# A recurrence's chunk products spread over earlier steps, its inverses moved to GpSimd alone, and copies moved from ScalarE to VectorE

## The chip, the cores and the metric

The kernel runs on one core of one Trainium2 chip. The metric is device time in microseconds (us); the profile adds one profiled execution of the program. PE is TensorE, PEld its weight loads, DVE VectorE, ACT ScalarE, POOL GpSimd, SP SyncE.

## The reference

Two stages. A recurrence over 768 time steps for 4 x 8 heads of dimension 40, then a small attention with four experts over its output.

```python
state = zeros((B, H, D, D))                     # B 4, H 8, S 768, D 40
for t in range(S):
    y[t] = einsum('bhd,bhde->bhe', r[t], state)
    Sa = einsum('bhde,bhe->bhd', state, a[t])
    state = state * w[t][:, :, None, :] - einsum('bhd,bhe->bhde', Sa, b[t]) \
            + einsum('bhd,bhe->bhde', v[t], k[t])
# then: top-2 gating of 4 experts; per expert causal softmax attention of width 64
# on q, k, v projections of y (width 320), and an output projection; weighted sum
```

Arithmetic is float32.

## The kernel before

**Chunks, groups, units.** The 768 time steps are cut into 24 chunks of 32. Four chunks make a group W (0 to 5). A unit is one chunk of eight heads (g = 0 to 3), so a group has 16 units and the recurrence 96, u = 0 to 95. Inside a chunk the recurrence is solved with small matrices: chunk products of decayed k and b (tile KB) with decayed a (tile AB) give strictly triangular 32x32 matrices; for the b part an inverse of (1 + that matrix) is needed for each head and chunk, 32 heads x 4 chunks = 128 of them in one group, one to a partition.

**Preparation, `prep(i)`**, i = 4W + g, makes for group W and eight heads: `a`, `b`, `c`, `s` (two scans on VectorE and two small instructions), `x`, `y` (A times the decay into AB, 512 elements each; `X`, `Y` are the same on GpSimd), `k`, `l` (the same for KB; `p` does both on GpSimd), `m`, `n` (chunk products on TensorE into PSUM, eight matrix products each, and a masking multiply on VectorE, L280, into GL), `d`, `q` (A's copies from AB into GL, L273), `o` (a store of GL's rows to DRAM, `Ld`), and `w`, `v`, `e` (loads of the next i's EW, EA, EK). In GL a group's 16 columns n = 4p + c are four chunks c for four pairs of heads p: `m` makes chunks 0 and 1, `n` chunks 2 and 3. GL has two buffers, so group W's products overwrite those of group W-2, whose units still read them (s_g, L362). EW, EA, EK have one buffer each after i = 7, AB four, KB ten.

**Inverse, `invert(w)`**: `ld` (`L`) loads MT, and a second copy of rows 11 to 30 into LT, from Ld; `cp` (`C`) sets the diagonal; `step` is one elimination step j of 30: a multiply (L309) and an add (L311) over m rows and 31 - j columns, m being the rows before row j. Rows 0 to 10 (KP = 11) are GpSimd's (list `tp`), the rest VectorE's (list `td`); LT lets GpSimd read row j unchanged. `st` (`S`) stores MT to DRAM (Td, L313), `bk` (`R`) loads it transposed into TT (L316, four loads). The inverse of group 0 has a split of its own.

**Order.** Every engine runs its instructions in the order in which the code emits them. A loop over steps n emits seven slots, one stage each of another unit: u (of unit n-1, the first user of TT), g (n), y (n-3), f (n-2), t (every other step), k, v. f's product is masked by VectorE (L383), which y of the next step needs; `decay` (L402) follows after slot 3. Preparation and inverse are put between by hand, in the tables SIDE, SIDE1 and SIDE2: the key is the step relative to n0 = 16(W-1), the slashes count slots, "1s" is `s` of g = 1, "t2" two instructions of `td`, L, C, S, R the inverse's parts (S, R and t count from n0 + 16). So group W is prepared while the units of group W-2 run, and inverted while those of W-1 run; u of group W's first unit needs TT. `tp` is spread over steps n0 + 4 to n0 + 12 (POOLT; to n0 + 10 for W = 1). SyncE issues nearly all DMAs in that same order. PSUM tiles `ps` go round over four buffers for u, g, f, v and the chunk products. W = 0 and i < 8 are done by START and EARLY.

Of the kernel before, what the change touches and what calls it, by code (L numbers as in the profile page):

```python
# [7 lines left out]
F32 = mybir.dt.float32  # L8
AF = mybir.ActivationFunctionType
# [25 lines left out]
    -13: "///1abc",  # L35
    -12: "///1s t1 1x t1",
    -11: "///1y t3/t2//1w",
    -10: "///1k t1 1l t1///1ve",
    -9: "///t1 2ab t1 2c/t2",
    -8: "///t1 2s t2 2x/t2//2w",  # L40
    -7: "///t1 2y t3/t2//2v",
    -6: "///2k t1 2l t2///2e",
    -5: "///3ab t1 3c t2",
    -4: "///3skl t1///3w",
    -3: "/S//3X/0m//0nodq",
    -2: "/R//3y/1m//1nodq 3v",
    -1: "/3e///2m//2nodq",
    0: "////3m//3nodq",
    1: "L",
    3: "C",  # L50
}

SIDE1 = {
    -11: "///t1",
    -10: "t1",
    -9: "t3///t2/t2",
    -8: "//t1/t1/t1",
    -7: "/t2/t1/t1/t2",
    -6: "//t1//t2",
    -5: "t1/t1//t1///t2",  # L60
    -4: "t1/t1//t2",
    -3: "///S/t1",
    -1: "/R",
    2: "L",
    6: "C",
}
SIDE2 = {
    -15: "///0abcs///0w",
    -14: "/0kly//0X///0ev",
    -13: "//1a/1bc",  # L70
    -12: "///t1 1s t1//1x",
    -11: "/t1//t1/t2//1w",
    -10: "///t1 1kl/t2/1y/1e",
    -9: "//2a/t1 2bc t1 2s/1v//t1",
    -8: "//t1/t1 2x/t3//2w",
    -7: "///t1 2y t3/2v t2",
    -6: "///2l t2 2k t1///2e",
    -5: "/t1/3a/3bc t1",
    -4: "///3k t1 3s/t1",
    -3: "/S 3Xw//0n/0m//0qo 3l",  # L80
    -2: "/0d/R/3y/1m/1n/1d 2q 3v",
    -1: "1o////3m 2m//2ndo",
    0: "/3e/1q/3q/3n//3do",
    1: "L",
# [52 lines left out]

def recurrence(tc, ctx, I, xT, CM, early, tail=None, KP=(11, 11, 11, 11, 11, 11)):
    nc = tc.nc
# [6 lines left out]
    def ps(shape):  # L146
        return pp.tile(shape, F32, name="ps", tag="ps", bufs=4)
# [23 lines left out]
    MT = ring("MT", [128, 32, 32], 1)[0]  # L171
    TP = [sp.tile([128, n], F32, name=f"TP{k}") for k, n in enumerate((220, 130))]
    TF = ring("TT", [128, 1032], 2)
# [73 lines left out]
    def prep(i):  # L247
# [24 lines left out]
        def f5(s):  # L272
            A.activation(gl[64:104, g, :, s, :], AB[64 * s:64 * s + 40, :, 32 * s:32 * s + 32], AF.Copy)  # L273
        def mm(c):
            p_a = ps([64, 4, 2, 64])
            for p in range(4):
                for cc in range(2):
                    n = p * 4 + c + cc
                    T.matmul(p_a[:, p, cc, :], kb[0:104, n, :], AB[0:104, n, :], start=True, stop=True)  # L279
            V.tensor_tensor(gl[0:64, g].rearrange("q (p c) s t -> q p c s t", p=4)[:, :, c:c + 2].rearrange("q p c s t -> q p (c s) t"),  # L280
                            p_a.rearrange("q p c (s t) -> q p (c s) t", s=2), maskn[:, None, None, :].to_broadcast([64, 4, 4, 32]),
                            op=OP.mult)
# [3 lines left out]
        def load(k):  # L286
            load_e(i + 1, k)
        return dict(a=f0a, b=f0b, c=f0c, s=f1, x=lambda: f2(0), X=lambda: f2(0, PL), y=lambda: f2(1), Y=lambda: f2(1, PL), p=fp, k=lambda: fk(0), l=lambda: fk(1),
                    d=lambda: f5(0), q=lambda: f5(1), m=lambda: mm(0), n=lambda: mm(2), o=f6,
                    w=lambda: load(0), v=lambda: load(1), e=lambda: load(2))  # L290

    def invert(w):
# [3 lines left out]
        def ld():  # L296
            nc.sync.dma_start(M, Ld[w % 2])
            nc.sync.dma_start(L, Ld[w % 2][:, kp:31])
        def cp():
# [18 lines left out]
        for j in range(1, 31):  # L318
            if w:
                tp += step(PL, j, 0, kp, TP[0])  # L320
                td += step(V, j, kp, 32, TP[1])
            else:
                x, y = (step(V, j, r, q, (TP[1], flat(KB[8]))[k]) for k, (r, q) in enumerate(((0, KS), (KS, kp))))
                td += x[:1] + y[:1] + x[1:] + y[1:]
                tp += step(PL, j, kp, 32, TP[0])
# [645 lines left out]
```

## Time and profile before

| | |
|---|---|
| time, median of 3 runs | 692.9 us (690.95 to 693.21) |
| the profiled execution | 693.37 us, its span 691.6 us, granted clock 0.933 |
| PE / DVE / ACT / POOL busy | 85% / 74% / 71% / 49% of the span |
| recurrence, units 0 to 95 | from 81.6 us to about 435 us |
| ACT A's copies, L273 | 48, 627 ns each |
| DVE chunk masks, L280 | 48, 64x512, 677 ns each |
| DMA | 82.09 MB, mean 119 GB/s |

The chain that ended last, as the profile follows it, lies wholly in the second stage; for the recurrence one reads windows and waits. A window row gives us, then the busy time of each engine with its count of instructions, then the granted clock, the DMA engines' share and GB/s. A waits row gives who waited for whom, us in total, times, longest. A timeline row gives start, duration, engine, line, operation and tiles, and in brackets the idle time before it and what ended it.

### The profile page before, as it was taken

The page shows a single profiled execution, that of the slowest core. Times are in us where ns is not written, and L with a number is a line of the kernel's source. Part 1 is how long each engine was busy: PE and PEld are TensorE (multiplying, and loading weights), DVE is VectorE, ACT ScalarE, POOL GpSimd, SP SyncE. Part 2 cuts the span into 40 slices and gives each one's busy share as a digit, 9 for nine tenths or more (in the row PEclk, how much of TensorE's full clock was granted, in tenths as well). Part 3 has the DMA queues.
Part 4 walks back from the last instruction along what each step waited for, and adds up shares of the span by engine and source line. Part 5 has one row for each costly group of instructions (what it writes and reads, how often), then busy time and mean ns, then how long its engine had stood idle before and what let it go on. Part 6 is the DMA issues. An engine that isn't in the chain of part 4 may idle for free. (4 is left out here: it accounts for less than half of the span.)

```text
span 691.6 us, 22423 instructions
## 1 busy us (share of the span) xinstructions
PE 585.3 (85%) x8849; PEld 510.3 (74%) x8849; DVE 515.0 (74%) x1248; ACT 492.2 (71%) x1311; POOL 336.8 (49%) x512
## 2 busy tenths in 40 slices
PE   5540587899789879968999999889989989999995
PEld 5540576797678779868988878778878877887774
DVE  8899869867976997798583675578887597667651
ACT  4593278789768977977899999447576666676762
POOL 5575469518824981785183010045456255333731
PEclk8555589999999999999999999989999999999998
DMA  7750654498477639855725892422231202202101
GB/s 219 208 146 14 140 142 118 125 204 208 112 140 204 159 102 192 213 129 112 198 69 127 251 235 69 144 75 58 77 91 34 77 23 77 77 11 53 42 30 44
DMA packets 89994, 82.09 MB, mean 119 GB/s; under 512 B 54936, under 2 KB 73112, under 8 KB 89880
## 3 DMA queue, kind: packets, MB, share of 16 engines
q1 hardware_dynamic: 89736, 80.47, 45.7%
q8 instruction: 72, 1.18, 0.8%
q14 instruction: 42, 0.34, 0.2%
q10 hardware_dynamic: 144, 0.10, 0.0%
HBM read 60.10 MB, written 14.16 MB: 107 GB/s over the span
## 5 line engine op out<-in xcount | busy, mean ns | idle before, releaser
L819 POOL TENSOR_TENSOR P<-P,m 128x128 f32<-128x128 f32 (+2 forms) x96 | 87.7, 935 | 97.4 <-DVE m L815 46.8
L390 PE MATMUL py<-R,LS 128*40 128x80 f32 x1536 | 82.5, 239 | 27.5 <-DVE R L383 20.1
L311 POOL TENSOR_TENSOR MT<-MT,TP 128x84 f32<-128x84 f32 (+13 forms) x169 | 88.1, 522 | 13.2
L390 PEld LDWEIGHTS py<-R,LS 128*40 128x40 f32 x1536 | 62.0, 119 | 35.9 <-DVE R L383 18.1
L279 PE MATMUL ps<-AB,KB 104*64 104x64 f32 x768 | 63.9, 251 | 23.8 <-DVE AB L266 8.4
L808 ACT ACTIVATE P<-sc,m 128x128 f32<-128x128 f32 (+2 forms) x96 | 60.7, 633 | 26.7 <-DVE m L807 21.4
L279 PEld LDWEIGHTS ps<-AB,KB 104*64 104x64 f32 x768 | 58.9, 164 | 27.5 <-issue 10.4
L807 DVE TENSOR_REDUCE m<-sc 128x1 f32<-128x128 f32 (+2 forms) x96 | 59.4, 622 | 22.3 <-PE sc L800 20.8
L383 DVE TENSOR_TENSOR R<-ps,CM 64x256 f32<-64x256 f32 x96 | 39.6, 413 | 45.8 <-PE ps L382 45.0
L364 ACT ACTIVATE GT<-ps 32x160 f32<-32x160 f32 x192 | 56.4, 294 | 20.5 <-PE ps L362 16.4
L797 PE MATMUL sc<-ks,qs 128*128 128x384 f32 (+4 forms) x256 | 63.2, 348 | 5.5 <-ACT P L808 5.3
L382 PE MATMUL ps<-RB,VU 128*64 128x64 f32 x768 | 63.3, 227 | 4.4 <-ACT VU L378 3.5
L382 PEld LDWEIGHTS ps<-RB,VU 128*64 128x64 f32 x768 | 54.2, 141 | 8.6 <-ACT VU L378 8.3
L372 ACT ACTIVATE R<-ps 32x160 f32<-32x160 f32 x192 | 56.5, 294 | 5.0 <-PE ps L370 1.8
L309 POOL TENSOR_TENSOR TP<-LT,MT 128x220 f32<-128x220 f32 (+9 forms) x100 | 56.2, 562 | 7.8
L827 PE MATMUL pt<-CM,P 128*128 128x128 f32 x336 | 52.9, 279 | 1.2 <-ACT pt L833 1.1
L400 ACT ACTIVATE R<-py 40x160 f32<-40x160 f32 x144 | 42.7, 297 | 13.5 <-PE py L390 10.4
L355 ACT ACTIVATE LS<-pt 64x320 f32<-64x320 f32 x96 | 41.5, 432 | 12.3 <-PE pt L351 10.9
L418 ACT ACTIVATE LS<-pt 40x320 f32<-40x320 f32 x92 | 39.6, 431 | 14.5 <-PE pt L414 12.8
L370 PE MATMUL ps<-GT,TT 128*33 128x40 f32 x1536 | 49.4, 207 | 0.5 <-ACT GT L364 0.2
L797 PEld LDWEIGHTS sc<-ks,qs 128*128 128x128 f32 x256 | 41.0, 191 | 10.6 <-ACT P L808 9.4
L719 PE MATMUL pt<-xh,wq 128*128 128x384 f32 x192 | 43.5, 363 | 3.6 <-POOL xh L698 1.5
(150 smaller groups left out, 1431.5 us busy)
## 6 DMA issues: line engine op xcount, KB each, us to landing
RB<-in_RB SPq DMA_DIRECT2D x24, 320.0 KB
EK<-in_EK SPq DMA_DIRECT2D x18, 416.0 KB
ks<-ks SPq DMA_DIRECT2D x32, 192.0 KB
R<-in_VG SPq DMA_DIRECT2D x24, 208.0 KB
EW<-in_EA SPq DMA_DIRECT2D x18, 214.5 KB
R<-in_VT SPq DMA_DIRECT2D x48, 80.0 KB
R<-in_RT SPq DMA_DIRECT2D x24, 160.0 KB
xT<-XT SPq DMA_DIRECT2D x48, 80.0 KB
```

Of the source, the lines that this page charges most:

```text
L279: T.matmul(p_a[:, p, cc, :], kb[0:104, n, :], AB[0:104, n, :], start=True, stop=True)
L309: return [lambda: e.tensor_tensor(tmp, row[:, None, :].to_broadcast([128, m, n]), M[:, r0:r0 + m, j][:, :, None].to_broadcast([128, m, n]) ...
L311: lambda: e.tensor_tensor(o, o, tmp, op=OP.add)]
L364: A.activation(gt[32 * g:32 * g + 32, s::2], p_g[64 * s:64 * s + 32], AF.Copy)
L372: A.activation(hd(r2[32:64, 40 * h0:40 * h0 + 320], 40)[:, s::2], p_u[64 * s:64 * s + 32], AF.Copy, scale=-1.0)
L382: T.matmul(p_f[:, 2 * p:2 * p + 2], vu[:, p, :], rb[:, 4 * g + p, :], start=True, stop=True)
L390: T.matmul(py[64 * s:64 * s + 40, p], ls[:, h, :], m, start=True, stop=True, tile_position=(0, 64 * s))
L797: T.matmul(ps[:, c, 0:cw], QS[b][:, e, o], KS[b][:, e, z, k], start=(z == 0), stop=(z == 1 and not last), skip_group_check=True)
L807: V.tensor_reduce(m[:, 0, t:t + 1], ps[:, 0:ch, 0:cw], axis=AX.XY, op=OP.max, negate=True)
L808: later(DE, lambda: A.activation(pv, ps[:, 0:ch, 0:cw], AF.Exp, bias=m[:, 0, t:t + 1], accum_out=m[:, 1, t:t + 1]))
L819: PL.tensor_tensor(P[:, 0:n], P[:, 0:n], m[:, 3, t:t + 1].to_broadcast([128, n]), op=OP.mult)
L827: T.transpose(p[:, 128 * y:128 * y + 128], st["P"][t][:, 128 * c:128 * c + 128], ident)
```

## The change

- The tables: of each preparation, `n` is split into `N` (chunk 2) and `M` (chunk 3), each with four products and a mask of 256 elements instead of one of 512. `m` goes to steps -12, -10, -7, -4, `N` to -6 to -3, `M` to -3 to 0 (before: `m`, `n` at -3 to 0). Some other parts move by a step or two, and the loads of the next EW, EA and EK by one to four steps; `3X` (GpSimd) becomes `3x` (VectorE). SIDE2 becomes the same as SIDE but for two early steps.
- `KP` of groups 1 to 5 is 31: GpSimd does all rows; `td` is empty, all `t` entries go, LT is not loaded for them. `S` and `R` stand at -2 and -1.
- A's copies `d`, `q` are done by VectorE from i = 8 on, and stand before `o`.

```diff
--- before.py
+++ after.py
@@ -33,54 +33,41 @@
     -15: "/0p//0xY///0v",
     -14: "//////0e",
     -13: "///1abc",
-    -12: "///1s t1 1x t1",
-    -11: "///1y t3/t2//1w",
-    -10: "///1k t1 1l t1///1ve",
-    -9: "///t1 2ab t1 2c/t2",
-    -8: "///t1 2s t2 2x/t2//2w",
-    -7: "///t1 2y t3/t2//2v",
-    -6: "///2k t1 2l t2///2e",
-    -5: "///3ab t1 3c t2",
-    -4: "///3skl t1///3w",
-    -3: "/S//3X/0m//0nodq",
-    -2: "/R//3y/1m//1nodq 3v",
-    -1: "/3e///2m//2nodq",
-    0: "////3m//3nodq",
+    -12: "///1s 0m 1x///1w",
+    -11: "///1y 1k 1l///1ve",
+    -10: "///2a 1m 2bc",
+    -9: "///2s 2x///2w",
+    -8: "///2y 2k 2l///2ve",
+    -7: "///3a 2m 3bc",
+    -6: "///3s 0N 3x///3w",
+    -5: "///3y 1N 3k 3l///3ve",
+    -4: "///2N 3m",
+    -3: "///0M 3N 0dqo",
+    -2: "///S 1Mdqo",
+    -1: "/R//2Mdqo",
+    0: "///3Mdqo",
     1: "L",
     3: "C",
 }
 
-SIDE1 = {
-    -11: "///t1",
-    -10: "t1",
-    -9: "t3///t2/t2",
-    -8: "//t1/t1/t1",
-    -7: "/t2/t1/t1/t2",
-    -6: "//t1//t2",
-    -5: "t1/t1//t1///t2",
-    -4: "t1/t1//t2",
-    -3: "///S/t1",
-    -1: "/R",
-    2: "L",
-    6: "C",
-}
+SIDE1 = {-2: "///S", -1: "/R", 2: "L", 6: "C"}
 SIDE2 = {
     -15: "///0abcs///0w",
     -14: "/0kly//0X///0ev",
-    -13: "//1a/1bc",
-    -12: "///t1 1s t1//1x",
-    -11: "/t1//t1/t2//1w",
-    -10: "///t1 1kl/t2/1y/1e",
-    -9: "//2a/t1 2bc t1 2s/1v//t1",
-    -8: "//t1/t1 2x/t3//2w",
-    -7: "///t1 2y t3/2v t2",
-    -6: "///2l t2 2k t1///2e",
-    -5: "/t1/3a/3bc t1",
-    -4: "///3k t1 3s/t1",
-    -3: "/S 3Xw//0n/0m//0qo 3l",
-    -2: "/0d/R/3y/1m/1n/1d 2q 3v",
-    -1: "1o////3m 2m//2ndo",
-    0: "/3e/1q/3q/3n//3do",
+    -13: "///1abc",
+    -12: "///1s 0m 1x///1w",
+    -11: "///1y 1k 1l///1ve",
+    -10: "///2a 1m 2bc",
+    -9: "///2s 2x///2w",
+    -8: "///2y 2k 2l///2ve",
+    -7: "///3a 2m 3bc",
+    -6: "///3s 0N 3x///3w",
+    -5: "///3y 1N 3k 3l///3ve",
+    -4: "///2N 3m",
+    -3: "///0M 3N 0dqo",
+    -2: "///S 1Mdqo",
+    -1: "/R//2Mdqo",
+    0: "///3Mdqo",
     1: "L",
     2: "////C",
 }
@@ -135,7 +122,7 @@
     return {"CM": cm}
 
 
-def recurrence(tc, ctx, I, xT, CM, early, tail=None, KP=(11, 11, 11, 11, 11, 11)):
+def recurrence(tc, ctx, I, xT, CM, early, tail=None, KP=(11, 31, 31, 31, 31, 31)):
     nc = tc.nc
     ep = early.enter_context(tc.tile_pool(name="early", bufs=1, side="right"))
     sp = ctx.enter_context(tc.tile_pool(name="rec", bufs=1))
@@ -169,7 +156,7 @@
     GL = [t[:, 0:4096].rearrange("p (g n s t) -> p g n s t", g=4, n=16, s=2) for t in GF]
     LT = ring("LT", [128, 20, 32], 1)[0]
     MT = ring("MT", [128, 32, 32], 1)[0]
-    TP = [sp.tile([128, n], F32, name=f"TP{k}") for k, n in enumerate((220, 130))]
+    TP = [sp.tile([128, n], F32, name=f"TP{k}") for k, n in enumerate((240, 130))]
     TF = ring("TT", [128, 1032], 2)
     TT = [t[:, 0:1024].rearrange("p (n t) -> p n t", n=32) for t in TF]
     LS = ring("LS", [128, 32, 40], 2)
@@ -270,15 +257,19 @@
         def fk(k):
             V.tensor_tensor(kb[0:104, :, 32 * k:32 * k + 32], EK.rearrange("p (n k c) -> p n k c", n=16, k=2)[:, :, k], sv[:, :, 1:33], op=OP.mult)
         def f5(s):
-            A.activation(gl[64:104, g, :, s, :], AB[64 * s:64 * s + 40, :, 32 * s:32 * s + 32], AF.Copy)
-        def mm(c):
-            p_a = ps([64, 4, 2, 64])
+            o, x = gl[64:104, g, :, s, :], AB[64 * s:64 * s + 40, :, 32 * s:32 * s + 32]
+            if i < 8:
+                A.activation(o, x, AF.Copy)
+            else:
+                V.tensor_copy(o, x)
+        def mm(c, m=2):
+            p_a = ps([64, 4, m, 64])
             for p in range(4):
-                for cc in range(2):
+                for cc in range(m):
                     n = p * 4 + c + cc
                     T.matmul(p_a[:, p, cc, :], kb[0:104, n, :], AB[0:104, n, :], start=True, stop=True)
-            V.tensor_tensor(gl[0:64, g].rearrange("q (p c) s t -> q p c s t", p=4)[:, :, c:c + 2].rearrange("q p c s t -> q p (c s) t"),
-                            p_a.rearrange("q p c (s t) -> q p (c s) t", s=2), maskn[:, None, None, :].to_broadcast([64, 4, 4, 32]),
+            V.tensor_tensor(gl[0:64, g].rearrange("q (p c) s t -> q p c s t", p=4)[:, :, c:c + m].rearrange("q p c s t -> q p (c s) t"),
+                            p_a.rearrange("q p c (s t) -> q p (c s) t", s=2), maskn[:, None, None, :].to_broadcast([64, 4, 2 * m, 32]),
                             op=OP.mult)
         def f6():
             nc.sync.dma_start(Ld[w % 2][32 * g:32 * g + 32].rearrange("n j t -> j n t"),
@@ -286,7 +277,7 @@
         def load(k):
             load_e(i + 1, k)
         return dict(a=f0a, b=f0b, c=f0c, s=f1, x=lambda: f2(0), X=lambda: f2(0, PL), y=lambda: f2(1), Y=lambda: f2(1, PL), p=fp, k=lambda: fk(0), l=lambda: fk(1),
-                    d=lambda: f5(0), q=lambda: f5(1), m=lambda: mm(0), n=lambda: mm(2), o=f6,
+                    d=lambda: f5(0), q=lambda: f5(1), m=lambda: mm(0), n=lambda: mm(2), N=lambda: mm(2, 1), M=lambda: mm(3, 1), o=f6,
                     w=lambda: load(0), v=lambda: load(1), e=lambda: load(2))
 
     def invert(w):
@@ -295,7 +286,8 @@
         kp = KP[w]
         def ld():
             nc.sync.dma_start(M, Ld[w % 2])
-            nc.sync.dma_start(L, Ld[w % 2][:, kp:31])
+            if kp < 31:
+                nc.sync.dma_start(L, Ld[w % 2][:, kp:31])
         def cp():
             PL.memset(M.rearrange("p t j -> p (t j)")[:, ::33], 1.0)
         def step(e, j, r0, r1, tmp):
@@ -318,7 +310,6 @@
         for j in range(1, 31):
             if w:
                 tp += step(PL, j, 0, kp, TP[0])
-                td += step(V, j, kp, 32, TP[1])
             else:
                 x, y = (step(V, j, r, q, (TP[1], flat(KB[8]))[k]) for k, (r, q) in enumerate(((0, KS), (KS, kp))))
                 td += x[:1] + y[:1] + x[1:] + y[1:]
@@ -439,23 +430,14 @@
     for W in range(1, NW):
         n0 = 16 * (W - 1)
         inv = invert(W)
-        td = list(inv["td"])
-        if W == NW - 1:
-            spread(n0 + 3, n0 + 12, 3, td)
-            td = []
         for r, line in {1: SIDE1, 2: SIDE2}.get(W, SIDE).items():
             for k, part in enumerate(line.split("/")):
                 for z in part.split():
-                    fs = []
-                    if z[0] == "t":
-                        fs, td = td[:int(z[1:])], td[int(z[1:]):]
-                    elif z == "S":
-                        fs, td = td + [inv["st"]], []
-                    elif z in "LCR":
-                        fs = [inv[{"L": "ld", "C": "cp", "R": "bk"}[z]]]
+                    if z in "LCSR":
+                        fs = [inv[{"L": "ld", "C": "cp", "S": "st", "R": "bk"}[z]]]
                     else:
                         fs = [P[4 * W + int(z[0])][x] for x in z[1:]]
-                    at(n0 + r + (16 if z[0] in "tSR" else 0), k, *fs)
+                    at(n0 + r + (16 if z in "SR" else 0), k, *fs)
         p0, p1 = POOLT.get(W, POOLT[0])
         spread(n0 + p0, n0 + p1, 0, inv["tp"])
 
```

## The prediction

> **What bounds the kernel now.** I read the page first, then the span by stage, then single steps, then the instructions of GpSimd and the DMA queue. The profiled execution took 693.37 us; the runs shown have a median of 692.9, so the sum below, made against 693.37, stands 0.5 above it.
>
> ```profile
> span 691.6 us, 22423 instructions
> PE 585.3 (85%) x8849; PEld 510.3 (74%) x8849; DVE 515.0 (74%) x1248; ACT 492.2 (71%) x1311; POOL 336.8 (49%) x512
> ```
>
> No engine is full on average, so the stages decide. The recurrence runs 96 units, 16 to a group of four chunks. I cut the span at the first u product of groups 0 to 5. Rows: us, then busy time of PE, PEld, DVE, ACT, POOL.
>
> ```profile
> 81.60:147.40 65.80, 56.34 (x1150) 51.60 (x1150) 53.54 (x115) 48.49 (x139) 36.20 (x63) 0.90 0.56 132
> 147.40:211.70 64.30, 55.69 (x1184) 50.13 (x1184) 49.42 (x114) 51.02 (x146) 39.05 (x65) 0.97 0.70 165
> 211.70:272.20 60.50, 54.19 (x1189) 48.75 (x1189) 50.95 (x114) 50.88 (x145) 38.07 (x64) 1.00 0.65 157
> 272.20:334.10 61.90, 53.76 (x1189) 48.61 (x1188) 48.68 (x110) 50.84 (x145) 38.37 (x64) 1.00 0.68 162
> 334.10:383.50 49.40, 47.31 (x1060) 41.45 (x1058) 28.62 (x79) 45.59 (x136) 25.03 (x61) 1.00 0.52 127
> ```
>
> Group 4 prepares nothing for a later group and takes 49.4. Groups 0 to 3 take 11 to 16 more; that surplus is what the change can touch. Where it lies shows when group 3 is set beside group 4, the same steps in each (steps 7 to 11, then the last four):
>
> ```profile
> 293.00:313.10 20.10, 14.45 (x334) 13.04 (x332) 19.49 (x41) 15.65 (x48) 17.98 (x28) 1.00 0.57 137
> 313.10:334.10 21.00, 19.13 (x394) 17.73 (x394) 14.89 (x37) 16.11 (x42) 7.56 (x17) 1.00 0.60 129
> 354.90:371.30 16.40, 15.30 (x335) 13.24 (x333) 11.23 (x31) 15.38 (x47) 13.73 (x35) 1.00 0.23 60
> 371.30:383.50 12.20, 11.84 (x266) 10.36 (x264) 4.23 (x13) 11.13 (x34) 0.26 (x2) 1.00 0.82 173
> ...
> PE py L390 <- DVE R L383: 4.3, 4, 2.3
> PE ps L362 <- ACT R L372: 1.4, 1, 1.4
> ```
>
> Steps 7 to 11 cost 20.1 - 16.4 = 3.7 more: DVE is busy 19.49 of 20.10 and TensorE waits for its mask (4.3 in the group). The last four cost 21.0 - 12.2 = 8.8 more: all 64 chunk products lie there, and ScalarE, busy with A's copies, holds TensorE 1.4. Together 12.5 = 61.9 - 49.4.
>
> **The change, part by part.** Durations of group 3 by line:
>
> ```profile
> L309 DVE TENSOR_TENSOR TP<-MT 128x19 f32<-128x19 f32 (+9 forms) x19 | 7.3, 384 | 0.4
> L311 DVE TENSOR_TENSOR MT<-MT,TP 128x19 f32<-128x19 f32 (+9 forms) x19 | 7.1, 372 | 0.4
> L383 DVE TENSOR_TENSOR R<-ps,CM 64x256 f32<-64x256 f32 x16 | 6.6, 411 | 3.4 <-PE ps L382 3.2
> L266 DVE TENSOR_TENSOR AB<-EA,SC 40x512 f32<-40x512 f32 x6 | 5.0, 839 | 1.1 <-DMA EA<-in_EA 1.0
> L280 DVE TENSOR_TENSOR GL<-ps,CM 64x512 f32<-64x512 f32 x7 | 4.7, 679 | 3.5 <-PE ps L279 3.4
> ...
> L273 ACT ACTIVATE GL<-AB 40x512 f32<-40x512 f32 x24 | 14.8, 626 | 8.4 <-DVE AB L266 7.6 <-POOL AB L266 0.4
> L696 DVE CAST xh<-x 128x1152 fp32r<-128x1152 f32 x7 | 5.3, 756 | 0.4 <-DMA x<-xT 0.3
> ```
>
> *VectorE* loses 38 inverse instructions a group, 7.3 + 7.1 = 14.4. It gains eight of A's copies; no row shows one, so between 512/1152 of the cast (0.34) and the 512-element mask (0.68); I take 0.45, nearest the cast, as it too is a copy from SBUF: 3.6. It gains the third mask part, 0.68 + 2 x 0.41 for 2 x 0.68, 0.14 x 4 = 0.6, and one A product from GpSimd (3x), 0.84. Net -9.4. *ScalarE* loses 8 x 0.626 = 5.0, and the 1.4 stall goes. The next possible delay is VectorE's queue, where the copies stand before the next unit's mask; the last four steps have room (14.89 busy of 21).
>
> *TensorE* does the same 64 products. Eight cost about 1.1 (8 blocks, 8.8, the surplus above). Moved over ten steps they can fill idle time: two steps where ScalarE is relieved of R's copies take 5.4, two ordinary ones 6.4:
>
> ```profile
> 334.10:339.50 5.40, 5.40 (x137) 5.03 (x135) 3.20 (x9) 4.63 (x14) 0.00 (x0) 1.00 0.59 143
> 358.50:364.90 6.40, 5.99 (x135) 5.18 (x134) 4.77 (x13) 6.00 (x19) 5.42 (x13) 1.00 0.28 63
> ```
>
> So 0.5 a step is free, 4.3 over nine. Left to its units alone a prepared group would take 49.4 + 8.8 - 4.3 = 53.9. Bounds: 49.4 (all hidden) and 58.2 (none).
>
> *GpSimd.* The inverse of a group keeps 60 instructions, but rows 11 to 30 join. Elements summed over j of m(31-j): 7,260 before, 9,920 after, 2,660 more.
>
> ```profile
> 282.50 0.24 POOL L309 TENSOR_TENSOR TP<-MT 128x30 f32<-128x30 f32 x1
> 295.00 1.56 POOL L309 TENSOR_TENSOR TP<-LT,MT 128x220 f32<-128x220 f32 x1
> 301.52 0.87 POOL L311 TENSOR_TENSOR MT<-MT,TP 128x187 f32<-128x187 f32 x1
> 320.49 0.22 POOL L311 TENSOR_TENSOR MT<-MT,TP 128x11 f32<-128x11 f32 x1
> 342.06 0.25 POOL L309 TENSOR_TENSOR TP<-MT 128x30 f32<-128x30 f32 x1
> 352.22 0.58 POOL L309 TENSOR_TENSOR TP<-LT,MT 128x220 f32<-128x220 f32 x1
> 354.24 0.59 POOL L311 TENSOR_TENSOR MT<-MT,TP 128x209 f32<-128x209 f32 x1
> 356.76 0.55 POOL L311 TENSOR_TENSOR MT<-MT,TP 128x187 f32<-128x187 f32 x1
> 371.41 0.22 POOL L311 TENSOR_TENSOR MT<-MT,TP 128x11 f32<-128x11 f32 x1
> ...
> 294.95 1.25 DVE L257 TENSOR_TENSOR_SCAN SUF<-EW,D 104x528 f32<-104x528 f32 x1
> 301.17 0.82 DVE L266 TENSOR_TENSOR AB<-EA,SC 40x512 f32<-40x512 f32 x1
> ```
>
> Group 4, with no preparation beside it: 342.06 to 371.63 = 29.6. From 11 to 209 elements an instruction grows by 0.37, 1.85 ns an element: 2,660 cost 4.9, so 34.5 alone. Group 3 took 282.50 to 320.71 = 38.2, 8.6 more. The rows show why: beside a scan (294.95) an instruction takes 1.56 for 0.58, 1.0 more; beside an A product (301.17) 0.87 for 0.55, 0.32 more. Five scans and ten products of preparation lay in that window: 5.0 + 3.2 = 8.2. VectorE's own inverse parts, present in group 4 too, show no such cost, so I give nothing back for them. The new window starts earlier in the group and holds six scans and twelve products, 6.0 + 3.8 = 9.8, and some six copies; a copy costs 0 to 0.48 (0.68 less the 0.2 of a smallest instruction), I take 0.2: 1.2. Sum D = 34.5 + 9.8 + 1.2 = 45.5 in groups 1 to 3. In group 0 the first scan precedes the window and two copies fall in it: 34.5 + 5.0 + 3.8 + 0.4 = 43.7. In group 4, 34.5.
>
> The Trainium skill, GPSIMD Engine Reference, Engine selection, advises VectorE for elementwise work on a tile and puts GpSimd at about twice its time for two inputs. By that, with the 679 ns mask as VectorE's price (1.3 ns an element), the 2,660 elements would cost about 7 us for my 4.9, and four inverses 8 us more than my sum, an estimate from that page.
>
> *The queue around it.* SyncE's issues (start, us):
>
> ```profile
> 278.75 0.34 SPq L297 DMA_DIRECT2D MT<-Ld  x1
> 320.74 0.34 SPq L313 DMA_DIRECT2D Td<-MT  x1
> 323.51 2.20 SPq L316 DMA_DIRECT2D TT<-Td  x4
> 335.08 0.32 SPq L284 DMA_DIRECT2D Ld<-GL  x1
> 337.40 0.34 SPq L297 DMA_DIRECT2D MT<-Ld  x1
> ...
> 341.98 0.16 POOL L300 MEMSET MT<- 128x32 f32 x1 [20.15 <-DMA MT<-Ld]
> 92.87 0.24 POOL L309 TENSOR_TENSOR TP<-MT 128x30 f32<-128x30 f32 x1 [3.49 <-DMA MT<-Ld]
> ```
>
> From the inverse's end, TT's last load is issued 4.6 to 5.0 later (to 325.71); a load like MT's takes 3.5 (278.75 to 282.26) to 4.6, Td's round 2.8. TT is there at about +7.6 (7.3 to 9). Behind TT's loads in SyncE's queue stand the last groups' o stores, a chunk load, then 3o and L: 3o at +6, L 2.3 later, the inverse's start 3.5 to 4.6 after L. GpSimd starts the next inverse at +13 (12 to 14). The dropped LT load (320 KB) takes an issue out of that queue. The E loads move one to four steps sooner with the products that free their tiles, two steps ahead of their use as now, and past S and R: VectorE's 1.0 for EA may stay, and I count it as nothing. Behind S's wait stand 1o, 2o, 3o, R and chunk loads needed three or more steps later; only 3o and R are on the loop, and both are counted in the 13 and the 7.6. S is now passed at step -2 instead of -3; where the inverse ends later than that, it makes no difference.
>
> So the inverses form a loop of their own: period D + 13 = 58.5, against 53.9 for the units. Before, it was 38.2 + 13 = 51 and hidden. It is now what ends last. Times of the groups' starts: group 1 at 92.87 + 43.7 + 7.6 = 144.2 (was 147.4). Group 2: the inverse starts at 136.6 + 13 = 149.6, ends 195.1, TT 202.7 (211.7). Group 3: 208.1, 253.6, 261.2 (272.2). Group 4: 266.6, 312.1, 319.7 (334.1). In group 4: 325.1 + 34.5 + 7.6 = 367.2, before the units' 319.7 + 49.4 = 369.1 (383.5). Gain 14.4; the rest of the program moves along unchanged. 693.4 - 14.4 = **679**.
>
> **The rivals.** *A, the inverse stays hidden.* If D is under 41, units decide. For it: VectorE, rid of its parts, may reach its scans outside GpSimd's way. Against: five scans cost 5.0 whatever else runs. The time: groups 1 to 3 gain 10.4, 6.6 and 8.0 against 53.9, group 0 about 8 (half its surplus of 16.4, the half in its later steps), or 33: 660. *B, the slower side: the inverse on GpSimd alone grows past the old period.* Break-even is D = 62.2 - 13 = 49.2 (mean of groups 1 to 3). If each copy blocks like a scan (1.0, not 0.2), D is 50.3; with 0.9 ns an element more for long, narrow tiles, 52.7. Then group 1 starts 0.8 later, groups 1 to 3 lose 3.5 each and group 4 half a us: 693 + 12 = 705; by the copies alone 695. The Trainium skill, SBUF — State Buffer, Who interferes with whom, says that an fp32 copy on VectorE can hold the ports that it shares with GpSimd for the whole instruction. No row of this trace shows one beside GpSimd. *C, no difference*: D near 49 puts the TT wait just where the products lay; 690.8 to 695. *D, VectorE becomes full* in steps 3 to 10, where a scan, products and a mask stand in nearly every step: 3.0 to 3.4 a step (a scan 1.25, a product or two at 0.84, a chunk mask 0.68, the unit's own 0.7) beside 16.4/5 = 3.3 of unit time; it would cost 1 to 3 a group, hidden while the loop's 58.5 decides.
>
> **How the numbers follow.** Loop-bound as forecast (668 to 688): 0.55. A (655 to 668): 0.19. Small gain to 690.8: 0.05. C: 0.08. B: 0.13. Faster by over 0.3% (2.1 us, about what a measurement here can tell): 0.79; same 0.08; slower 0.13. Range 661 to 695: it leaves out A's lower end and B's upper, some 0.17.
>
> **What would show it.** Right: GpSimd's inverse lasting 45 in groups 1 to 3 and 34 in group 4; TensorE's u products at groups 2 to 4 waiting some 4 us for DMA TT<-Td; the waits for L383 and L372 gone; group 4 still 49.4. If u never waits for TT, A holds; if the inverse passes 49, B. The forecast is wrong also if TensorE waits for VectorE's masks in steps 4 to 11 longer than the 4.3 shown.

## The result and the profile after

The changed kernel takes 700.25 us (median of 9 runs, 696.02 to 703.48), the kernel before 693.21 (9 runs, 689.73 to 695.27). The ratio is 1.010, with an interval of 1.007 to 1.013: about 1% slower, where 2% faster was forecast. The profiled execution took 701.92 us. These two lines of its page stand against the two of before in the prediction; VectorE and ScalarE do less, GpSimd more, as the change says.

```profile
span 699.9 us, 22331 instructions
PE 587.9 (84%) x8849; PEld 513.8 (73%) x8849; DVE 475.3 (68%) x1110; ACT 471.8 (67%) x1279; POOL 366.4 (52%) x508
```

The same cut by groups (columns as before), and as a last row the end of group 3, its step 15:

```profile
81.70:147.80 66.10, 53.81 (x1149) 48.98 (x1150) 49.83 (x90) 44.72 (x133) 45.62 (x64) 0.91 0.54 129
147.80:212.10 64.30, 55.41 (x1184) 50.38 (x1184) 43.59 (x89) 45.82 (x136) 45.38 (x63) 0.92 0.66 156
212.10:275.00 62.90, 55.72 (x1184) 50.67 (x1184) 43.26 (x89) 45.80 (x136) 44.92 (x63) 0.93 0.61 154
275.00:337.80 62.80, 54.99 (x1184) 49.98 (x1184) 40.84 (x85) 45.81 (x136) 41.11 (x61) 0.93 0.59 145
337.80:391.80 54.00, 48.76 (x1056) 42.78 (x1057) 13.54 (x40) 45.81 (x136) 30.02 (x61) 0.97 0.42 111
...
327.90:337.80 9.90, 3.41 (x77) 3.12 (x76) 3.68 (x10) 3.50 (x10) 1.16 (x3) 0.81 0.79 147
```

Groups 0 to 4 took 66.1, 64.3, 62.9, 62.8 and 54.0, where they had taken 65.8, 64.3, 60.5, 61.9 and 49.4. Added up, the last group starts at 391.8 instead of 383.5, 8.3 later; the profiled executions differ by 8.55. More than half of it, 4.6, is in group 4, which prepares nothing. The last row shows where a prepared group loses time: the step before the next group's first unit takes 9.90, and TensorE works in 3.41 of them. The waits name the cause:

```profile
PE ps L361 <- DMA TT<-Td: 31.6, 5, 8.1
...
POOL MT L292 <- DMA MT<-Ld: 50.1, 5, 16.2
```

TensorE's u product waits 31.6 us for TT, 8.1 at most, once for each group 1 to 5. Behind it is the loop that was forecast: the inverse, the round over DRAM to TT, the last store, the load of MT, the next inverse. GpSimd, SyncE's queue and TensorE around the end of group 3 (timelines; start, duration):

```profile
283.66 0.24 POOL L301 TENSOR_TENSOR TP<-MT 128x30 f32<-128x30 f32 x1
328.97 0.26 POOL L303 TENSOR_TENSOR MT<-MT,TP 128x30 f32<-128x30 f32 x1
...
329.26 0.34 SPq L305 DMA_DIRECT2D Td<-MT  x1
329.70 0.38 SPq L275 DMA_DIRECT2D Ld<-GL  x1
332.05 2.31 SPq L308 DMA_DIRECT2D TT<-Td  x4
334.46 0.84 SPq L275 DMA_DIRECT2D Ld<-GL  x1
335.40 1.04 SPq L397 DMA_DIRECT2D xT<-XT  x2
336.53 0.60 SPq L325 DMA_DIRECT2D R<-in_VT  x1
337.22 0.37 SPq L275 DMA_DIRECT2D Ld<-GL  x1
...
340.05 0.71 SPq L288 DMA_DIRECT2D MT<-Ld  x1
...
337.83 0.42 PE L361 MATMUL ps<-GT,TT 128*33 128x40 f32 x6 [6.53 <-DMA TT<-Td]
345.39 0.16 POOL L292 MEMSET MT<- 128x32 f32 x1 [16.16 <-DMA MT<-Ld]
```

The inverse runs from 283.66 to 329.23, 45.57. S follows at once (329.26), the four TT loads of R at 332.05, and TensorE's u at 337.83, 8.6 after the inverse's end. Behind the TT loads SyncE issues 2o, two stores of xT, a load of tile R and 3o (337.22, 8.0 after the end), then L at 340.05 (10.8); the next inverse starts at 345.46, 16.2 after the end of the last.

Group 4 loses time at both ends. At its start TensorE works without a pause, but its first two steps take 6.80 where the same steps took 5.40 before (row 334.10:339.50 in the prediction): the granted clock is 0.77 of full speed in them, against 1.00.

```profile
337.80:344.60 6.80, 6.77 (x134) 6.38 (x135) 2.52 (x8) 3.75 (x12) 0.00 (x0) 0.77 0.78 203
```

In windows of one us the clock is 0.50 from 335 to 340, so it fell while TensorE waited for TT and came back about 3 us after TensorE had started again. That is 1.4 of the 4.6. At its end, group 4's inverse and queue read so:

```profile
379.76 0.27 POOL L303 TENSOR_TENSOR MT<-MT,TP 128x30 f32<-128x30 f32 x1
...
381.10 0.31 SPq L327 DMA_DIRECT2D R<-in_VT  x1
...
382.38 0.34 SPq L305 DMA_DIRECT2D Td<-MT  x1
387.46 2.14 SPq L308 DMA_DIRECT2D TT<-Td  x4
...
391.81 0.52 PE L361 MATMUL ps<-GT,TT 128*33 128x40 f32 x16 [3.10 <-DMA TT<-Td]
```

The inverse has ended at 380.03, but its store S is issued at 382.38, 2.35 later: in SyncE's queue it stands behind a chunk load that waits for y of step -2 (381.10) and two more. From S to the first TT load it takes 5.1, where 2.8 was enough in group 3, and u waits 3.10 for TT. With the 1.4 of the start this is 4.5 of the 4.6.

### The profile page after: what moved, and what is told of

Same layout as the page of the kernel before. It is cut to its first block, busy times and chain, and to the rows that moved or that the text cites. A ratio compares the mean times of both kernels' runs of the same rounds, so it can differ in the third digit from the quotient of the medians.

```text
span 699.9 us, 22331 instructions
## 1 busy us (share of the span) xinstructions
PE 587.9 (84%) x8849; PEld 513.8 (73%) x8849; DVE 475.3 (68%) x1110; ACT 471.8 (67%) x1279; POOL 366.4 (52%) x508
## 5 line engine op out<-in xcount | busy, mean ns | idle before, releaser
L801 POOL TENSOR_TENSOR P<-P,m 128x128 f32<-128x128 f32 (+2 forms) x96 | 87.6, 934 | 95.4 <-DVE m L797 51.1
L301 POOL TENSOR_TENSOR TP<-MT 128x84 f32<-128x84 f32 (+13 forms) x169 | 104.5, 618 | 18.3 <-DMA MT<-Ld 5.4
L303 POOL TENSOR_TENSOR MT<-MT,TP 128x84 f32<-128x84 f32 (+13 forms) x169 | 106.2, 629 | 13.2
L381 PE MATMUL py<-R,LS 128*40 128x80 f32 x1536 | 86.5, 242 | 5.6 <-DVE R L374 2.9
L270 PE MATMUL ps<-AB,KB 104*64 104x64 f32 x768 | 66.1, 253 | 24.0 <-DVE AB L253 7.9
L270 PEld LDWEIGHTS ps<-AB,KB 104*64 104x64 f32 x768 | 61.0, 167 | 26.3 <-issue 9.1
L363 ACT ACTIVATE R<-ps 32x160 f32<-32x160 f32 x192 | 56.5, 294 | 34.8 <-PE ps L361 31.6
L361 PE MATMUL ps<-GT,TT 128*33 128x40 f32 x1536 | 50.0, 211 | 31.6 <-DMA TT<-Td 31.6
L381 PEld LDWEIGHTS py<-R,LS 128*40 128x40 f32 x1536 | 65.3, 121 | 12.9 <-ACT LS L409 5.6
L373 PE MATMUL ps<-RB,VU 128*64 128x64 f32 x768 | 65.2, 230 | 5.1 <-ACT VU L369 4.1
L361 PEld LDWEIGHTS ps<-GT,TT 128*33 128x33 f32 x1536 | 37.6, 117 | 40.9 <-issue 32.8
L373 PEld LDWEIGHTS ps<-RB,VU 128*64 128x64 f32 x768 | 54.8, 143 | 10.8 <-ACT VU L369 9.6
L809 PE MATMUL pt<-CM,P 128*128 128x128 f32 x336 | 51.9, 276 | 2.3 <-ACT pt L815 1.8
```

The source lines that it names most:

```text
L301: return [lambda: e.tensor_tensor(tmp, row[:, None, :].to_broadcast([128, m, n]), M[:, r0:r0 + m, j][:, :, None].to_broadcast([128, m, n]) ...
L303: lambda: e.tensor_tensor(o, o, tmp, op=OP.add)]
L361: T.matmul(p_u[64 * s:64 * s + 33, p], tt[:, o:o + 33], gt[:, h, :], start=True, stop=True, tile_position=(0, 64 * s))
L363: A.activation(hd(r2[32:64, 40 * h0:40 * h0 + 320], 40)[:, s::2], p_u[64 * s:64 * s + 32], AF.Copy, scale=-1.0)
L373: T.matmul(p_f[:, 2 * p:2 * p + 2], vu[:, p, :], rb[:, 4 * g + p, :], start=True, stop=True)
L381: T.matmul(py[64 * s:64 * s + 40, p], ls[:, h, :], m, start=True, stop=True, tile_position=(0, 64 * s))
```

## Experiments

Theory 1 is the forecast's: the loop of inverse and queue ends last, and its parts add up. Its rivals differ from run to run: that VectorE or the units' own time decides, that the other parts of the change cost the time, and, from the fifth run on, theory 2: that the place of S and R in SyncE's queue does. All edits are against the changed kernel, but for the second one. D is the time of an inverse, E its end.

### The parts, each without another

**The inverse split again** between GpSimd and VectorE, all else as changed.

```diff
-def recurrence(tc, ctx, I, xT, CM, early, tail=None, KP=(11, 31, 31, 31, 31, 31)):
+def recurrence(tc, ctx, I, xT, CM, early, tail=None, KP=(11, 11, 11, 11, 11, 11)):
...
+                td += step(V, j, kp, 32, TP[1])
...
+        spread(n0 + 4, n0 + 13, 3, inv["td"])
```

> Everything as in the changed kernel, but the inverses of groups 1 to 5 are shared again (rows 0 to 10 GpSimd, 11 to 31 VectorE, VectorE's part spread evenly over steps n0+4 to n0+13). Theory 1 (the loop of inverse and its DMA rounds ends last, about 16.4 + D a group): GpSimd's inverse falls from 45.6 to about 40.5, TensorE's waits for TT fall from 31.6 in all to under 12, time 678 to 688. Rival (the spread products and VectorE's copies are what costs): time stays at 698 or above, with VectorE's mask as what TensorE waits for.

Measured: 732.66 against 691.96, ratio 1.058 (1.051 to 1.065). GpSimd's part fell to 37.3 to 38.9 in groups 0 to 3, yet S came 8.5 to 15.2 after its end, waiting for VectorE's part. Waits, and the window of group 3:

```profile
PE ps L270 <- DVE KB L258: 27.4, 10, 3.7
297.10:368.60 71.50, 59.64 (x1184) 54.79 (x1185) 52.52 (x123) 45.81 (x136) 33.53 (x62) 0.88 0.55 133
```

The early products need their KB, which VectorE makes, in steps where rows of the inverse stand in its queue. The time is the rival's, but TensorE waits for KB, and for TT 18.0, not for masks. The miss is one of theory 1's: shortening GpSimd's part does not shorten the loop when VectorE's part ends it. Only this even spread of VectorE's part was tried.

**The inverse on GpSimd alone in the kernel before**, its products, copies and queue unchanged.

```diff
-def recurrence(tc, ctx, I, xT, CM, early, tail=None, KP=(11, 11, 11, 11, 11, 11)):
+def recurrence(tc, ctx, I, xT, CM, early, tail=None, KP=(11, 31, 31, 31, 31, 31)):
...
-            nc.sync.dma_start(L, Ld[w % 2][:, kp:31])
+            if kp < 31:
+                nc.sync.dma_start(L, Ld[w % 2][:, kp:31])
...
-                td += step(V, j, kp, 32, TP[1])
```

> The kernel before with one part of the change alone: groups 1 to 5 inverted by GpSimd alone, the products at steps -3 to 0 and A's copies on ScalarE as before. Theory 1: D about 43 (34.5 alone, 8.6 for scans and products beside it), a loop of about 60 a group against groups of 60 to 64 before, so part of what VectorE gains is kept: 681 to 690, TensorE waiting 1 to 4 for TT in a group. Rival (GpSimd's longer inverse is a loss in itself): 698 or above.

Measured: 713.66, ratio 1.030 (1.024 to 1.037), the rival's side. D is 45.8, 46.9, 46.5, 43.2, 34.6. Its waits:

```profile
PEld ps L279 <- POOL AB L266: 21.6, 7, 6.1
PE ps L279 <- POOL AB L266: 14.4, 5, 5.9
```

The product 3X, which the change gives to VectorE, here stands behind the longer inverse on GpSimd; the last products and with them L come late, and the next inverse starts 19 to 22.7 after E. So the parts of the change need each other: either alone, placed as here, costs 3 to 6%.

### The terms of D

**One scan of each preparation left out** (the first of the two, SUF, of i = 8 and later; run twice, and D is read in the second run).

```diff
         def f0a():
+            if i > 7:
+                return
             V.tensor_tensor_scan(SUF[:, 0:528][:, ::-1], EW[:, ::-1], d1[:, ::-1], 1.0, op0=OP.mult, op1=OP.add)
```

> The changed kernel without the first scan (L257 of before, SUF) from i = 8 on; the later instructions read what the tile held, so outputs differ. Theory 1 with the port between VectorE and GpSimd as the price of D: three scans fewer in each window at 1.0 each, D 45.6 -> 42.6, and the loop passes it on: each of groups 1 to 3 and group 0 2 to 3 shorter, 688 to 692. Rival (the inverse's length is its instructions alone, or TensorE's wait has another cause): D stays at 45 or the time within 2 of the changed kernel.

> The kernel without the first scan from i = 8 on once more (later instructions read what the tile held, so outputs differ), for a profile of GpSimd's inverse. If VectorE's scans beside it lengthen it by 1.0 each, D of groups 1 to 3 is 42.6 to 43.5 against 45.6 to 46.5; if not, 45 or above.

Measured: 689.43 and 690.26, ratios 0.9964 (0.9933 to 0.9994) and 0.9985 (0.9953 to 1.0017). Both times lie in theory 1's range. D fell to 42.4, 42.9, 41.8, 42.3, by 3.2 to 4.2 for three scans beside an inverse (four in group 1), 0.9 to 1.4 each: about the 1.0 that the forecast read from one row. Group 4, without scans, kept 34.55. TensorE still waits 21.7 for TT.

**A's copies back on ScalarE**, at their new places.

```diff
-            if i < 8:
+            if i < 24:
                 A.activation(o, x, AF.Copy)
```

> The changed kernel with A's copies back on ScalarE. Theory 1: a copy on VectorE costs GpSimd's inverse 0 to 0.2, four to six of them stand in a window, so D falls by 0.3 to 1.0 and the time by 0 to 4: 696 to 700. Rival (a copy holds GpSimd like a scan, 1.0 each): D falls by 4 or more and the time by 12 or more.

Measured: 701.57, ratio 1.012 (1.007 to 1.017), no different from the change whole. D fell by 1.3, 1.0, 1.0 and 1.8, 1.3 in the mean, which for six copies would be the 0.2 each of the forecast. But in two of these four inverses one scan fewer also stands beside GpSimd. The changed kernel's rows show less: GpSimd goes on beside a copy, and its instructions lose little against those of the same size in group 4 (the last row).

```profile
327.90 0.87 DVE L264 COPY GL<-AB 40x512 f32<-40x512 f32 x2
...
327.92 0.57 POOL L303 TENSOR_TENSOR MT<-MT,TP 128x58 f32<-128x58 f32 x1
379.04 0.31 POOL L303 TENSOR_TENSOR MT<-MT,TP 128x58 f32<-128x58 f32 x1
```

This pair, 0.26, is the largest loss; beside the six copies of group 3 the losses add up to some 0.6, 0.1 each. Rival B's 1.0 each is excluded either way.

### Where the rest of the loop is

**Elimination steps 21 to 30 left out**, in groups 1 to 5.

```diff
-                tp += step(PL, j, 0, kp, TP[0])
+                tp += step(PL, j, 0, kp, TP[0]) if j < 21 else []
```

> The changed kernel with elimination steps 21 to 30 left out of GpSimd's inverse in groups 1 to 5 (20 instructions, some 10 us of each inverse; outputs differ), all else unchanged. Theory 1 (the loop of inverse and DMA rounds, and nothing else of the change, makes the groups long): D about 34.5, loop about 51, TensorE's waits for TT near 0, and the time that of the units alone, 702 - 31.6 = 670, so 664 to 675. Rival (the spread products or VectorE's copies cost too, the waits for TT only hide it): 685 or above.

Measured: 684.79, ratio 0.988 (0.980 to 0.995): theory 1's range is missed, and the time lies just under the rival's 685. D fell by some 12, to 34.3 (24.1 in group 4), but TensorE still waited 16.7 for TT. In group 3 (timelines):

```profile
305.58 0.61 POOL L303 TENSOR_TENSOR MT<-MT,TP 128x220 f32<-128x220 f32 x1
...
310.81 0.31 SPq L327 DMA_DIRECT2D R<-in_VT  x1
...
312.47 0.34 SPq L305 DMA_DIRECT2D Td<-MT  x1
...
317.33 2.29 SPq L308 DMA_DIRECT2D TT<-Td  x4
```

The inverse ends at 306.19, S is issued 6.3 later and R 4.9 after S. Theory 1 as it stood could not say that: an inverse that ends sooner only waits for its place in the queue, which TensorE's progress sets. From here theory 2 is on trial. S came 4.5 to 7.3 after E in groups 0 to 3, and 13.3 in group 4.

**S two slots sooner in step -2**, ahead of the chunk loads there, in all groups.

```diff
-    -2: "///S 1Mdqo",
+    -2: "/S//1Mdqo",
...
```

> The changed kernel with the inverse's store S two slots earlier in step -2, ahead of three chunk loads in SyncE's queue. Theory 1: in group 4, where those loads held S 2.4 after the inverse's end and TT came 11.8 after it, TT comes 8 after it and TensorE's wait of 3.1 goes; the other groups unchanged. Time 2 to 4 less than the changed kernel, 696 to 699. Rival (the loads, now behind S, come late for their units): no gain or a loss, with TensorE waiting for RB or R.

Measured: 704.46, ratio 1.015 (1.007 to 1.024): a miss. Group 4 gained 2.1 (54.0 to 51.9, S now 0.02 after E), but in groups 0 to 3 u came 9.0 to 10.4 after E, against 7.2 to 9.0. TensorE waits for TT there, not for RB or R, so the rival's reason isn't the one. The chunk loads now stand between S and R, and the TT loads take longer to issue (end of group 1; 2.24 there in the changed kernel):

```profile
203.66 0.34 SPq L305 DMA_DIRECT2D Td<-MT  x1
204.10 0.38 SPq L327 DMA_DIRECT2D R<-in_VT  x1
204.53 0.69 SPq L328 DMA_DIRECT2D RB<-in_RB  x1
...
206.53 3.99 SPq L308 DMA_DIRECT2D TT<-Td  x4
```

**S and R a step sooner in the last inverse alone** (-3 and -2, ahead of the chunk loads).

```diff
+                    if z in "SR" and W == NW - 1:
+                        at(n0 + 16 + {"S": -3, "R": -2}[z], 1, *fs)
+                        continue
```

> The changed kernel with S and R of the last inverse alone (W = 5) a step earlier, where the kernel before had them (steps -3 and -2, slot 1). In group 4 nothing is prepared and GpSimd ends early; theory 2 (the place of S and R in SyncE's order, behind chunk loads that wait for TensorE, is a second cost of the change, and all of group 4's loss): group 4 falls from 54.0 to about 50, the time by 3 to 4.5, to 695.5 to 697.5. Rival (TT is late there because GpSimd's inverse ends late): no difference.

Measured: 694.59 against 692.85, ratio 1.001 (0.999 to 1.004). That is a little better than forecast. S follows E by 0.03, no wait for TT is left at the end of group 4, and the group takes 51.7. Its window, and that of its first two steps:

```profile
332.50:384.20 51.70, 49.60 (x1056) 43.67 (x1056) 13.53 (x40) 44.67 (x134) 30.03 (x61) 0.95 0.43 113
332.50:340.20 7.70, 7.70 (x134) 7.26 (x134) 2.52 (x8) 3.73 (x12) 0.61 (x4) 0.64 0.70 186
```

So theory 2 has half of group 4's loss, not all of it. What is left, 51.7 - 49.4 = 2.3, are its first two steps, 7.70 for 5.40, with TensorE busy throughout at a granted clock of 0.64. They follow a wait of 6.74 for TT. By the ratios (1.010 to 1.001) some 6 us came back. 2.3 of them are group 4's; groups 0 and 1, whose places the edit leaves alone, were 1.3 and 2.4 shorter in this profiled execution. That part is not explained by the edit.

**Both: the short inverse with S and R at -3 and -2 in all groups.**

```diff
-                tp += step(PL, j, 0, kp, TP[0])
+                tp += step(PL, j, 0, kp, TP[0]) if j < 21 else []
...
+                    if z in "SR" and True:
+                        at(n0 + 16 + {"S": -3, "R": -2}[z], 1, *fs)
+                        continue
```

> The shortened inverse (steps 21 to 30 left out in groups 1 to 5; outputs differ) with S and R of all groups at steps -3 and -2, slot 1, as before the change. Theory 2: the 3.3, 3.3, 3.4, 3.9 and 2.7 that TensorE still waited for TT with the short inverse alone go, 684.8 -> 668 to 674, which is then the time of the units alone. Rival (they wait for DMA bandwidth, not for the place in the queue): 680 or above.

Measured: 672.95, ratio 0.970 (0.966 to 0.974), as theory 2 said. The row for TT is gone from the waits. Groups 3 and 4:

```profile
259.50:317.90 58.40, 54.87 (x1188) 49.83 (x1187) 42.76 (x91) 45.84 (x137) 32.95 (x43) 0.97 0.66 159
317.90:367.40 49.50, 47.40 (x1058) 41.39 (x1058) 14.13 (x42) 45.80 (x137) 21.15 (x41) 1.00 0.46 122
```

Groups 0 to 3 take 59.0, 60.0, 58.8 and 58.4. Group 4, at clock 1.00 and with no wait for TT ahead of it, takes the 49.5 of its units. This is about what the kernel would take with the inverse hidden, 20 us under before, and here it took an inverse about 12 us shorter than GpSimd's own.

### Shorter queue, with the whole inverse

**The earlier S of above, the stores of xT two steps later, and the second preparation's scans one and two steps sooner, ahead of the inverse**; and then the same with **two of the four TT loads on ScalarE's queue**.

```diff
-    -14: "//////0e",
-    -13: "///1abc",
-    -12: "///1s 0m 1x///1w",
+    -14: "///1abcs///0e",
+    -12: "///0m 1x///1w",
...
-                if cw == 3:
+                def store():
...
+                        at(u + 5, 6, store)
```

```diff
+        def bq():
+            for g in range(2, 4):
+                A.dma_start(TT[w % 2][32 * g:32 * g + 32], Td[w % 2][32 * g:32 * g + 32].rearrange("n t j -> t n j"))
```

> e6 and two more: the stores of xT (two DMAs in each of the last four units of a group) go two steps later in SyncE's queue, behind L; and the two scans of g = 1 go one and two steps earlier, ahead of the inverse. Theory 1: 3o and L 1 sooner, one or two scans less beside GpSimd, D 44: loop 2 to 3.5 shorter in groups 1 to 3, 685 to 692 in all. Rival (the loop's length is set by DMA landing times, not by the queue): as e6.

> e7 with two of TT's four loads issued from ScalarE's queue at the end of step 0. Theory 1: the issue of four loads, 2.3 on one queue, halves; TT about 1 sooner for each of five groups: 680 to 688. Rival (ScalarE, waiting for Td, holds up the units' copies): 690 or above.

Measured: 698.06, ratio 1.007 (1.003 to 1.010), and 704.23, 1.016 (1.008 to 1.024): both miss, and the second lies on the rival's side. In time, that is; ScalarE did not wait for Td. It reached its two loads only behind its own work, 6.5 after SyncE's were issued, and group 4 took 59.6, where the version with SyncE alone took 51.1.

```profile
382.83 2.11 SPq L307 DMA_DIRECT2D TT<-Td  x2
389.35 0.34 ACTq L310 DMA_DIRECT2D TT<-Td  x1
389.73 0.59 ACTq L310 DMA_DIRECT2D TT<-Td  x1
```

**The last inverse's S and R early and the stores later**, and that **with the earlier scans**, S and R elsewhere as in the change.

> The same without the earlier scans. If two scans taken from beside the inverse are worth what the trace showed (1.0 each, three groups), it is 3 to 6 above n11; if the inverse is as long as before, within 2 of it.

> The changed kernel with three edits that only move work: the last inverse's S and R a step earlier, the stores of xT two steps later, the scans of g = 1 ahead of the inverse; copies stay on VectorE. If SyncE's queue sets the part of the loop that lies between inverses: GpSimd starts 1 to 2 sooner after the last inverse than the 16.2 to 17.7 of the changed kernel, groups 1 to 3 take 60 to 61, and the time is 686 to 691, below both kernels. If DMA landing sets it: as with the last inverse's S and R alone, 694.

Measured: 695.99, ratio 1.003 (1.001 to 1.005), and 694.08, 1.001 (0.998 to 1.003), against 693.83. The second time is what was expected if the landing of the DMAs sets the loop, not the queue. The groups of its profiled execution (689.87) say more: 1 to 3 take 60.3, 61.0 and 61.3, as expected if the queue does, and the next inverse starts 13.3, 14.9, 17.4 and 15.6 after E. So the 13 of the forecast is reached once in four. In the third round R is issued 6.0 after E instead of 2.8, waiting for S to land; why S lands late there is not settled. TensorE still waits 19.6 for TT.

The scans did not get out of the way: six stand beside each inverse of groups 1 to 3 in both versions, so the two times say nothing of a scan's price. And the later stores cost something that no expectation counted: VectorE may not write XT again before the store has landed.

```profile
DVE XT L392 <- DMA xT<-XT: 5.5, 3, 4.6
```

The 4.6 lies in the last group. From its first u to its last it takes 50.7 in this version, 48.5 before and 49.8 in the changed kernel; in the other versions with the later stores 51.2 to 53.4, but for the one with two queues (49.5).

### Another split

**16 rows on GpSimd, the rest on VectorE in its idle steps**, with the last group early, later stores and earlier scans; once with A's copies on ScalarE, once on VectorE. And the **inverse on GpSimd with A's copies on ScalarE** and the same three edits.

```diff
-def recurrence(tc, ctx, I, xT, CM, early, tail=None, KP=(11, 31, 31, 31, 31, 31)):
+def recurrence(tc, ctx, I, xT, CM, early, tail=None, KP=(11, 16, 16, 16, 16, 16)):
...
+        for r, k, c in ((5, 6, 4), (7, 6, 4), (8, 6, 2), (10, 6, 4), (11, 6, 2), (13, 6, 8), (14, 2, 4)):
+            at(n0 + r, k, *td[:c])
...
```

> A version made from the readings: the changed kernel with copies on ScalarE, the stores of xT two steps later, the scans of g = 1 earlier, the last inverse's S and R a step earlier, and rows 16 to 31 of the inverses of groups 1 to 5 back on VectorE (28 small instructions, put where VectorE has idle time). D 42 to 43, loop about 58.5 in groups 1 to 3 (62.8 in the changed kernel), group 4 50: 680 to 690. Rival (VectorE is full again, as with rows 11 to 31): 695 or above.

> The version with the stores of xT, the g = 1 scans and the last S and R moved and copies on VectorE, with rows 16 to 31 of the inverses on VectorE, placed where its queue was idle (steps 5, 7, 10, 12, 13, 14). D 43, so 60 - 2 = 58 to 59 a group if VectorE keeps pace: 682 to 688. If VectorE is the next to be full, 692 or above.

> The same without the return of rows to VectorE (GpSimd alone). D 44.5 to 45.5, loop 61 in groups 1 to 3, group 4 50: 688 to 695; what it has over the sixteen-row version is the price of 2 us of D in each group.

Measured: 700.75, ratio 1.011 (1.007 to 1.015); 698.08, 1.009 (1.006 to 1.013); and 692.22, 1.000 (0.997 to 1.003). In the first D is 41.7 to 43.7 in groups 0 to 3 and TT waits are nearly gone (3.6), yet groups 1 to 3 take 62.7 to 63.2. VectorE is busy 46 to 48 us of them and ScalarE 50 to 52; that this is the reason is argued, not shown. The last group, with its wait for a store of xT, takes 53.4. In the second, group 3's window has VectorE at 49.00 of 62.20, and S comes 1.9 to 3.7 after GpSimd's part in groups 1 to 3, waiting for VectorE's rows:

```profile
272.70:334.90 62.20, 55.16 (x1186) 49.93 (x1187) 49.00 (x115) 45.93 (x136) 40.14 (x62) 0.97 0.59 151
```

The third has the fewest waits for TT of the versions with a whole inverse on GpSimd alone, 5.0, and is as fast as before. It was expected to be slower than the sixteen-row version by the price of 2 us of D in a group, and is 8.5 faster. None of the versions that compute everything is faster than before beyond its interval. The third without the later stores, whose wait costs it some of its last group (51.4), was not run.

## Why the prediction was wrong, step by step

- **What ends last: right.** The inverses form the loop; u waits for TT at every group; the waits for L383 and L372 of before are down from 20.1 and 4.3 to under 3.
- **D: right, and nearly term by term.** 45.55, 46.50, 46.04, 45.57 and 34.57 where 43.7, 45.5 three times and 34.5 stood. Set beside the same sizes in group 4, group 3's instructions lose 6.2 to six scans, 4.3 to twelve products and some 0.6 to six copies, where the forecast had 6.0, 3.8 and 1.2; the last two errors cancel. Group 1, 1.0 over, had a seventh scan beside it. Group 0, 1.85 over, had six scans and six copies, not five and two. Beside a scan (the last row) GpSimd takes 1.59 for 238 elements; the instruction of the same size before it, which stood beside a product of KB, took 0.94:

```profile
304.68 0.94 POOL L301 TENSOR_TENSOR TP<-MT 128x238 f32<-128x238 f32 x1
305.70 1.59 POOL L303 TENSOR_TENSOR MT<-MT,TP 128x238 f32<-128x238 f32 x1
...
305.61 1.24 DVE L244 TENSOR_TENSOR_SCAN SUF<-EW,D 104x528 f32<-104x528 f32 x1
```

- By the ratio of about two (the Trainium skill, GPSIMD Engine Reference, Engine selection), with the mask as VectorE's price, four inverses were estimated to cost 8 us more, 2 each. The 34.57 of group 4, where 34.5 stood, excludes that estimate here. An fp32 copy on VectorE can hold the ports that it shares with GpSimd for the whole instruction (the Trainium skill, SBUF — State Buffer, Who interferes with whom). This trace doesn't show it: GpSimd loses some 0.1 beside a copy of 0.4 to 0.6.
- **E to the next inverse, "+13 (12 to 14)": the step that failed.** Measured 16.3, 16.6, 17.7 and 16.2. 3o came at 7.4 to 9.4, not 6; L 2.8 to 3.3 after it, not 2.3; the inverse 5.0 to 5.8 after L, not 3.5 to 4.6. In the three rounds that count this is 3.3 + 3.6 + 4.7 = 11.6. More than half of it, 1.4 + 1.9 + 3.4 = 6.7, is 3o's. The forecast left out the two stores of xT ahead of 3o and priced the issues as in a free queue, 0.3 to 0.4; in the rows above the stores take 1.04, the o store before them 0.84 and the load of tile R, the chunk load that it did count, 0.60. In the third round the inverse's R came 1.7 late, waiting for S to land. The other 5 or so are landing times, which the forecast took from the kernel before: 3o takes 0.6 to 1.0 more in each round, the load of MT 0.4 to 1.2 more than the 4.6. Why they land later is not shown.
- **With the real 16.7, rival B's break-even is D = 62.2 - 16.7 = 45.5**, and 46.0 came in the mean of groups 1 to 3. The loop of 62 to 63 replaced groups of 60.5 to 64.3: no gain could come of it in groups 1 to 3, and there the traces differ by 3.3.
- **"S is now passed at step -2 instead of -3; where the inverse ends later than that, it makes no difference": failed where the inverse ends sooner**, in group 4. The chunk loads that stand ahead of S at the new place, which the forecast does not name, wait there for TensorE. Group 4 took 54.0 for 49.4: 4.6. Of this 3.1 is the wait for TT at its end. The other 1.4 is a cost that the forecast has nowhere: the first two steps after the wait for TT run at a lower granted clock. With S and R moved the first was gone and the second was 2.3; with the short inverse and S and R early both were gone, and group 4 took 49.5. In groups 0 to 3 the short inverse showed the same hold on S.
- **Smaller terms.** The first inverse started at 95.02, not 92.87: 2.15. D: 1.85 + 1.0 + 0.5 + 0.1 = 3.45. E to u ended at 8.6, not 7.6: 1.0. Sum of all: 11.6 + 4.6 + 2.15 + 3.45 + 1.0 = 22.8; the last group was forecast for 369.1 and began at 391.8, 22.7 later.
- **The units' time, 53.9: too low, and hidden.** Without its wait for TT group 3 takes 62.8 - 6.5 = 56.3, and with no wait for TT groups 0 to 3 take 58.4 to 60.0 (the short inverse with S early). So at the forecast's period of 58.5 the loop would not have ended 4.6 behind the units; the two would have been about level. Rival A's 660 could not have come: about 673 is the least that it could give.
- **The signs.** "Group 4 still 49.4" was not there, and pointed to the right place. The u products of groups 2 to 4 waited 7.6, 6.2 and 6.5 for TT, where "some 4" stood.

## What to carry to other kernels

Work moved to an engine that is off the bound closes a loop through whatever hands its result on; sum the whole loop. Price each DMA issue in it by rows from a full queue (here up to 0.93), not by a free one (0.34), and take landing times from a stretch that is as busy. When TensorE has waited, look at the clock of the steps behind the wait before calling them slow for another reason. For each step moved in a hand-written order, look at what stands ahead of it in the queue in every group, above all in the one where its producer finishes sooner. Parts of a change that free each other's engines are not worth their parts' sum: here either half alone, as placed, cost 3 to 6%, and both together 1%. When a store is moved later, ask who must wait for it to land.

## What was not expected of the hardware

- SyncE's issue of one load or store took 0.31 to 0.42 in a free queue, and 0.34 to 0.93 in the stretch between R and L of the changed kernel. The four TT loads took 2.1 to 2.4 there, and 3.7 to 4.0 with S two slots sooner, where three chunk loads and, in groups 0 to 3, a store went just ahead of them. By what mechanism an issue grows, the runs don't show.
- TensorE's granted clock was 0.50 for 7 to 10 us around each of the four longest waits for TT (6.2 to 8.1) in the changed kernel, and the u product behind such a wait took 0.75 instead of 0.48. In group 4 it cost 1.4, and 2.3 with the last S and R early. The traces show wait and clock together; what lowers the clock they don't show.
- VectorE's copies of 40x512 take 0.5 (0.62 into the tile GLe), and GpSimd loses some 0.1 beside each:

```profile
L264 DVE COPY GLe<-AB 40x512 f32<-40x512 f32 x16 | 9.8, 615 | 0.4
L264 DVE COPY GL<-AB 40x512 f32<-40x512 f32 x16 | 7.9, 495 | 0.4
```
